# Inverted denominators of a linear attention, spread to 128 partitions by two DMAs per row block instead of four to 32 partitions each

## The chip, the cores and the metric

The kernel runs on one core of one Trainium2 chip. The metric is device time in microseconds (us): the time from the start to the end of one execution, median of several. A profile of one execution is shown beside it; its span runs from the first to the last instruction.

## The reference

One transformer block with adaptive layer norm, on 2048 rows of 1024 (bfloat16 in and out): a linear attention with 32 heads of 32, then a gated MLP of width 3584.

```python
mod = (silu(c) @ w_mod).reshape(1, 6, 1, -1)        # sa, ca, ga, sb, cb, gb
h = layernorm(x) * (1 + ca) + sa
q, k, v = heads(h @ wqkv)                            # 32 heads of 32
phi = lambda t: where(t > 0, t + 1, exp(t)) + 1e-6
pq, pk = phi(q), phi(k)
kv = einsum('bhsd,bhse->bhde', pk, v)
z = einsum('bhsd->bhd', pk)
num = einsum('bhqd,bhde->bhqe', pq, kv)
den = einsum('bhqd,bhd->bhq', pq, z)[..., None] + 1e-6
x = x + ga * ((num / den) merged @ wo)
h = layernorm(x) * (1 + cb) + sb
x = x + gb * ((gelu(h @ w_gate) * (h @ w_up)) @ w_down)
```

What the change touches is the division by `den`: one number for each row and head.

## The kernel before

The rows are worked in four blocks of 512 (`TG`), numbered 0 to 3; blocks 0 and 1 are pair 0, blocks 2 and 3 pair 1. Many of the products are done in seven half-size products instead of eight (the functions built on `seven`), with sums and differences of the operands made on VectorE.

Stages, in program order: layer norm and the products for v and k of all blocks (`kvq_phase`), which leave kv and z summed over all rows; the products for q of pair 0 and then of pair 1 (`q_stages`), which leave phi(q) in `pqT[b]`, laid out as 128 partitions (4 heads of 32 dimensions) by 8 head groups (`KD`) by 512 rows; `merge_phase`, in which kv is multiplied into `wo` (`wp_step`, one head group at a time) beside the last q stages; `wo_phase`, the output projection with the residual: eight row tiles of blocks 0 and 1 by plain products (`wo_tile`, line 1519, 16 matmuls a tile), then blocks 2 and 3 by seven-product stages (`wo_stages`, line 1583), and the second layer norm; then gate, up and down of the MLP for rows 0 to 1023 and 1024 to 2047 (`gate_up`, lines 1698 and 1709, and `down_out`, lines 1914 and 1959).

The division is done on q's side. `den_sums` makes, for a pair of blocks, the denominators of all heads by small matmuls with z (line 1271), takes the logarithm and then the exponential of its negative on ScalarE (lines 1273 and 1274), and stores the inverted denominators (`rdc`, bfloat16) by four DMAs of 16 KB on SP's queue into a DRAM tile, `den_scr` (line 1279). `den_mul` reads them back for one block, so that all 32 partitions of a head hold the same row (line 1289), into an 8 KB buffer per partition, `rden`, and multiplies `pqT[b]` by it in four VectorE instructions of two head groups each. The buffers come from `rden_ring`: blocks 0, 1 and 2 use the same one, block 3 another. The projections wait for these multiplications. All VectorE products and sums of two tensors are issued by the helper `tt_op`, so the profile puts them on line 779.

Nothing is issued in program order. Every instruction is recorded by a planner (`Plan`), with its engine, an assumed cost and what it depends on. The planner orders each engine's instructions by list scheduling with due times; for TensorE it keeps the program's order. `plan.extra` adds to the assumed latency of a DMA, and `plan.together(True)` lets several writes into the same memory lines wait only for the older users of the lines and not for one another. At the end `refine` moves the instructions of each engine by a table written out in the file, `SHIFTS`: one number for each instruction of an engine, which says from which place of the planner's order the one in this place comes (`z4` stands for four zeros). The order that runs is the one after `SHIFTS`.

SP's queue carries nearly all loads: weights, x, the reads of den, and the transposing loads of the second layer norm's rows (`h2_load`, line 1455). POOL's queue carries most stores to DRAM.

Of the kernel before, what the change touches and what calls it, by code (L numbers as in the profile page):

```python
# [11 lines left out]
BF16 = mybir.dt.bfloat16  # L12
# [9 lines left out]
        "z1 4 4 4 4 4 -5 -5 -5 -5 48 -1 -1 -1 -1 -1 -1 -1 -1 -1 -1 -1 -1 -1 -1 -1 -1 7 7 7 7 7 7 7 7 7 7 7 7 7 7 7 7 "  # L22
        "-17 -17 -17 -17 -17 -17 -17 -17 3 3 3 3 -5 -5 -5 -5 8 8 8 8 20 20 20 20 20 20 20 20 20 20 20 20 20 20 20 20 "
        "-20 -20 -20 -20 24 24 24 24 24 24 24 24 24 24 24 24 24 24 24 24 -28 -28 -28 -28 -28 -28 -28 -28 -44 -44 -44 "
        "-44 16 16 16 16 -36 -36 -36 -36 12 12 12 12 12 12 12 12 12 12 12 12 -8 -8 -8 -8 -36 -36 -36 -36 28 28 28 28 "
        "-40 -40 -40 -40 -4 -4 -4 -4 z16 -20 -20 -20 -20 z12 16 16 16 16 16 16 16 16 16 16 16 16 16 16 16 16 16 16 16 "
        "16 16 16 16 16 16 16 16 16 16 16 16 16 -24 -24 -24 -24 -24 -24 -24 -24 -40 -40 -40 -40 -40 -40 -40 -40 8 8 8 8 "
        "8 8 8 8 8 8 8 8 8 8 8 8 -16 -16 -16 -16 -16 -16 -16 -16 z8 16 16 16 16 16 16 16 16 16 16 16 16 16 16 16 16 -16 "
        "-16 -16 -16 -16 -16 -16 -16 8 8 8 8 52 -21 -21 -21 -21 -21 -21 -21 -21 -1 -1 -1 -1 -1 -1 -1 -1 11 11 11 11 11 "
        "11 11 11 28 28 28 28 19 19 19 19 11 11 11 11 20 20 20 20 -25 -25 -25 -25 -25 -25 -25 -25 -25 -25 -25 -25 8 8 8 "  # L30
        "8 8 8 8 8 25 25 25 25 25 25 25 25 13 13 13 13 -37 -37 -37 -37 -37 -37 -37 -37 -3 -3 -3 -3 25 25 25 25 25 25 25 "
        "25 25 25 25 25 25 25 25 25 -32 -8 -8 -8 -8 -32 -32 -32 -32 -40 -40 -40 -40 -16 -16 -16 -16 -12 -12 -12 -12 -20 "
        "-20 -20 -20 40 40 40 40 z4 -8 -8 -8 -8 -4 -4 -4 -4 -4 -4 -4 -4 -4 -4 -4 -4 20 20 20 20 -4 -4 -4 -4 -12 -12 -12 "
        "-12 -8 -8 -8 -8 -8 -8 -8 -8 -8 -8 -8 -8 36 36 36 36 -4 -4 -4 -4 -4 -4 -4 -4 z4 4 4 4 4 -12 -12 -12 -12 -8 -8 "
        "-8 -8 4 4 4 4 8 8 8 8 8 8 8 8 -12 -12 -12 -12 16 16 16 16 z4 12 12 12 12 12 12 12 12 -36 -36 -36 -36 -8 -8 -8 "
        "-8 -16 -16 -16 -16 12 12 12 12 4 4 4 4 -4 -4 -4 -4 8 8 8 8 -16 -16 -16 -16 -4 -4 -4 -4 4 4 4 4 -4 -4 -4 -4 z8 "
        "4 4 4 4 -4 -4 -4 -4 4 4 4 4 -4 -4 -4 -4 z16 4 4 4 4 24 24 24 24 24 24 24 24 -4 -4 -4 -4 -4 -4 -4 -4 -20 -20 "
        "-20 -20 28 28 28 28 20 20 20 20 32 32 32 32 -20 -20 -20 -20 -20 -20 -20 -20 -20 -20 -20 -20 -12 -12 -12 -12 "
        "-12 -12 -12 -12 -12 -12 -12 -12 28 28 28 28 4 4 4 4 -12 -12 -12 -12 -12 -12 -12 -12 16 16 16 16 -4 -4 -4 -4 "
        "-12 -12 -12 -12 12 12 12 12 -8 -8 -8 -8 z4 -20 -20 -20 -20 16 16 16 16 16 16 16 16 16 16 16 16 -8 -8 -8 -8 12 "  # L40
        "12 12 12 -12 -12 -12 -12 -24 -24 -24 -24 8 8 8 8 -20 -20 -20 -20 -4 -4 -4 -4 4 4 4 4 -4 -4 -4 -4 4 4 4 4 -4 -4 "
        "-4 -4 4 4 4 4 -4 -4 -4 -4 z8 32 32 32 32 32 32 32 32 32 32 32 32 -12 -12 -12 -12 -8 -8 -8 -8 -8 -8 -8 -8 -20 "
        "-20 -20 -20 60 60 60 60 60 60 60 60 -16 -16 -16 -16 -24 -24 -24 -24 8 8 8 8 8 8 8 8 8 8 8 8 -28 -28 -28 -28 "
        "-36 -36 -36 -36 -16 -16 -16 -16 -24 -24 -24 -24 8 8 8 8 -12 -12 -12 -12 -12 -12 -12 -12 -12 -12 -12 -12 -12 "
        "-12 -12 -12 12 12 12 12 12 12 12 12 12 12 12 12 12 12 12 12 -24 -24 -24 -24 -12 -12 -12 -12 12 12 12 12 -24 "
        "-24 -24 -24 16 11 11 11 11 -9 -9 -9 -9 -9 -9 -9 -9 9 9 9 9 z5 -14 -14 -14 -14 z24 6 6 6 6 -2 -2 -2 -2 -8 -8 "
        "z10 6 6 6 6 -4 -4 -4 -4 -4 -4 2 2 2 2 2 2 2 2 -8 1 1 1 1 1 1 7 7 7 7 -18 6 6 6 6 -8 -8 -8 -8 2 -9 -9 11 11 11 "
        "11 -4 z4 1 -9 -9 -9 -9 1 1 1 1 -9 32 32 32 32 32 32 32 32 32 32 32 32 32 32 32 32 48 48 48 48 48 48 48 48 24 "
        "24 24 24 -28 -28 -28 -28 -28 -28 -28 -28 -28 -28 -28 -28 -28 -28 -28 -28 -28 -28 -28 -28 4 4 4 4 4 4 4 4 4 4 4 "
        "4 -40 -40 -40 -40 -40 -40 -40 -40 -40 -40 -40 -40 z8 64 64 64 64 4 4 4 4 4 4 4 4 -12 -12 -12 -12 -12 -12 -12 "  # L50
        "-12 4 4 4 4 4 4 4 4 -12 -12 -12 -12 -12 -12 -12 -12 -4 -4 -4 -4 -4 -4 -4 -4 -4 -4 -4 -4 -4 -4 -4 -4 4 4 4 4 4 "
        "4 4 4 -12 -12 -12 -12 -12 -12 -12 -12 z16 8 8 8 8 8 8 8 8 -8 -8 -8 -8 -8 -8 -8 -8 4 4 4 4 -4 -4 -4 -4 z8 44 44 "
        "44 44 24 24 24 24 -8 -8 -8 -8 -8 -8 -8 -8 -4 -4 -4 -4 -12 -12 -12 -12 -4 -4 -4 -4 -12 -12 -12 -12 -8 -8 -8 -8 "
        "16 16 16 16 8 8 8 8 -12 -12 -12 -12 -12 -12 -12 -12 -12 -12 -12 -12 4 4 4 4 -4 -4 -4 -4 8 8 2 2 2 2 4 4 4 4 4 "
        "4 4 4 -14 -14 -14 -14 8 8 8 8 8 8 8 8 -4 -4 -4 -4 -12 -12 -12 -12 20 20 20 20 -4 -4 -4 -4 -4 -4 -4 -4 12 12 12 "
        "12 24 24 -2 -2 -2 -2 -10 -10 -10 -10 10 10 10 10 -22 -22 -22 -22 8 8 32 32 -6 -6 -6 -6 6 6 -16 -16 -16 -16 22 "
        "22 z2 -8 -8 -8 -8 -4 -4 -4 -4 z2 -6 -6 -6 -6 z2 -6 -6 -6 -6 z4 6 6 -2 -2 -2 -2 -2 -2 6 6 6 6 -2 -2 -2 -2 4 4 4 "
        "4 -12 -12 38 38 8 8 8 8 34 34 -4 -4 -4 -4 8 8 4 4 -14 -14 -22 -22 -6 -6 -6 -6 -2 -2 -2 -2 8 8 -22 -22 20 20 20 "
        "20 -6 -6 -12 -12 -12 -12 -10 -10 -10 -10 z6 4 4 4 4 -14 -14 -14 -14 z6 12 12 12 12 -4 -4 -4 -4 32 32 32 32 8 8 "
        "8 8 -12 -12 -12 -12 -12 -12 32 32 -8 -8 -8 -8 -18 -18 8 8 24 24 -2 -2 -12 -12 -12 -12 -12 -12 -12 -12 6 6 6 6 "  # L60
        "z2 -16 -16 -16 -16 8 8 8 8 z4 6 6 6 6 z2 4 4 4 4 4 4 -30 -30 -30 -30 30 30 30 30 -2 -2 -2 -2 10 10 10 10 z2 -4 "
        "-4 -16 -16 -12 -12 -12 -12 24 24 4 4 -4 -4 16 16 -6 -6 -6 -6 -20 -20 -20 -20 z6 12 12 -12 -12 -12 -12 -2 -2 -2 "
        "-2 -2 -2 -2 -2 4 4 -2 -2 -2 -2 6 6 6 6 -4 -4 -4 -4 26 26 26 26 2 2 -10 -10 z6 26 26 -14 -14 -14 -14 22 22 2 2 "
        "-6 -6 -6 -6 -6 -6 -16 -16 -16 -16 z2 -6 -6 -6 -6 8 8 8 8 -8 -8 -8 -8 -4 -4 -4 -4 z2 6 6 6 6 36 36 -2 -2 -8 -8 "
        "-8 -8 z2 -4 -4 26 26 -4 -4 4 4 4 4 -4 -4 30 30 -6 -6 24 24 -16 -16 -16 -16 -4 -4 z2 -12 -12 -12 -12 -10 -10 "
        "-10 -10 2 2 2 2 -4 -4 -10 -10 -10 -10 50 50 -2 -2 -2 -2 2 2 -4 -4 -4 -4 -2 -2 -2 -2 -2 -2 4 4 4 4 30 30 -8 -8 "
# [430 lines left out]
def kernel(  # L497
# [14 lines left out]
    P = 128  # L512
# [6 lines left out]
    KD = D // P  # L519
    JF = F // P  # L520
    TG = 512
# [1664 lines left out]
```

## Time and profile before

| | before |
|---|---|
| median of 3 runs | 738.85 us (738.4 to 741.09) |
| the profiled execution | 740.71 us |
| its span | 738.9 us |
| TensorE (PE) busy | 719.7 us, 97% |
| VectorE (DVE) busy | 655.2 us, 89% |
| ScalarE (ACT) busy | 451.6 us, 61% |
| GpSimd (POOL) busy | 97.8 us, 13% |
| DMA | 159.26 MB in 160956 packets, mean 216 GB/s |
| granted TensorE clock | 1.0 throughout |

PE is matmul and PEld the weight load, which overlaps it. In a timeline a line gives the start and the length in us, the engine, the line of the kernel, the operation, out<-in by tile names, and the number of instructions; the bracket is the idle time just before the first of them and what ended it. The chain of waits follows the work that ended last back from the end, step by step, to what released it; "DMA mem<-den" in it is the time from the issue of a read of den to its landing in SBUF, "DMA den<-mem" that of a store. In the windows view each engine has its busy time and instruction count for a stretch; the last three columns are the granted clock, the mean busy share of the 16 DMA engines, and GB/s.

### The profile page before, as it was taken

How to read it: one execution, taken by the hardware profiler on the slowest of the kernel's cores; microseconds unless marked ns; L12 is line 12 of the kernel's file. 1: busy time of each engine (PE TensorE's matmuls, PEld its weight loads, DVE VectorE, ACT ScalarE, POOL GpSimd, SP SyncE). 2: the span in 40 equal slices, each digit the busy share in tenths (PEclk: the TensorE clock that was granted, in tenths of full speed). 3: DMA queues.
4: the chain of work that ended last, by engine and by line, in shares of the span. 5: the costliest groups of instructions: out<-in, count | busy, mean ns of one | idle time of the engine just before them, and what ended most of it. 6: DMA issues, size and time to landing. Idle time of an engine off the chain costs nothing.

```text
span 738.9 us, 12098 instructions
## 1 busy us (share of the span) xinstructions
PE 719.7 (97%) x4341; PEld 404.2 (55%) x4353; DVE 655.2 (89%) x1469; ACT 451.6 (61%) x823; POOL 97.8 (13%) x174
## 2 busy tenths in 40 slices
PE   4999999999999999999999999999999999999997
PEld 3444444444344455555555576545555555568674
DVE  6799978787789999998998798888898999999998
ACT  4385665669787789999777631017667766753110
POOL 2345542020020101213100000101000000000000
PEclk9999999999999999999999999999999999999999
DMA  9977886986799685666795898753334546599982
GB/s 296 363 209 223 207 156 127 339 283 179 243 271 258 209 279 194 192 203 229 235 202 173 228 288 244 273 186 114 114 91 153 185 161 207 157 240 302 262 270 73
DMA packets 160956, 159.26 MB, mean 216 GB/s; under 512 B 34176, under 2 KB 140416, under 8 KB 160256
## 3 DMA queue, kind: packets, MB, share of 16 engines
q1 hardware_dynamic: 143696, 122.57, 55.9%
q0 software_dynamic: 14848, 33.82, 15.4%
q10 hardware_dynamic: 2352, 2.10, 0.9%
q8 instruction: 34, 0.56, 0.3%
q14 instruction: 26, 0.21, 0.1%
HBM read 122.42 MB, written 36.04 MB: 214 GB/s over the span
## 4 chain that ended last, share of the span: by engine, by line
PE 79%; DVE 12%; DMA 4%; ACT 2%; SPq 1%; issue 1%; DVEq 0%; ACTq 0%
PE psum L1698 33%; PE psum L1959 11%; PE psum L1709 11%; PE psum L1914 9%; DVE mem L779 8%; PE psum L1142 5%; PE psum L1583 3%; PE psum L1212 3%; DMA mem<-den 3%; PE psum L915 2%; DVE mem L857 2%; DMA den<-mem 1%; DVE mem L1062 1%; DVE mem L1081 1%; PE psum L1256 1%
## 5 line engine op out<-in xcount | busy, mean ns | idle before, releaser
L779 DVE TENSOR_TENSOR mem<-mem 128x512 f16<-128x512 f16 (+13 forms) x857 | 376.5, 485 | 15.5 <-DMA mem<-den 4.3
L1698 PE MATMUL psum<-mem 128*128 128x512 f16 x1144 | 275.0, 379 | 0.2
L1086 ACT ACTIVATE mem<-psum 128x512 f32<-128x512 f32 (+3 forms) x320 | 169.0, 556 | 131.8 <-PE psum L1959 45.2
L779 DVE TENSOR_TENSOR mem<-psum,mem 128x512 f16<-128x512 f32 (+5 forms) x213 | 159.3, 756 | 26.9 <-PE psum L1142 5.4
L1698 PEld LDWEIGHTS <-mem 128*128 128x128 f16 (+1 forms) x1144 | 111.8, 98 | 101.3 <-issue 1.5
L1709 PE MATMUL psum<-mem 128*128 128x256 f16 x742 | 108.4, 273 | 0.0
L1709 PEld LDWEIGHTS <-mem 128*128 128x128 f16 (+1 forms) x742 | 72.2, 98 | 44.9 <-DVE psum L779 0.7
L1959 PE MATMUL psum<-mem 128*128 128x256 f16 (+1 forms) x784 | 88.0, 273 | 0.0
L1959 PEld LDWEIGHTS <-mem 128*128 128x128 f16 x784 | 76.7, 98 | 11.7
L1914 PE MATMUL psum<-mem 128*128 128x512 f16 (+2 forms) x348 | 74.9, 370 | 0.6 <-DVE mem L779 0.5
L1142 PE MATMUL psum<-mem 128*128 128x512 f16 (+1 forms) x274 | 62.4, 379 | 0.4
L779 DVE TENSOR_TENSOR psum<-psum,mem 128x256 f32<-128x256 f32 x106 | 44.6, 427 | 13.4 <-ACT mem L1086 12.0
L1914 PEld LDWEIGHTS <-mem 128*128 128x128 f16 x350 | 34.2, 98 | 36.2 <-issue 0.7
L1212 PE MATMUL psum<-mem 128*128 128x512 f16 x224 | 51.7, 379 | 1.5 <-DVE mem L779 1.3
L1142 PEld LDWEIGHTS <-mem 128*128 128x128 f16 x280 | 27.1, 98 | 31.8 <-issue 0.6
L1754 ACT ACTIVATE psum<-psum 128x512 f32<-128x512 f32 x56 | 32.6, 585 | 11.8 <-PE psum L1709 7.7
L1773 ACT ACTIVATE mem<-psum 128x512 f16<-128x512 f32 x56 | 33.1, 598 | 9.1 <-PE psum L1698 9.1
L1715 ACT ACTIVATE psum<-psum 128x256 f32<-128x256 f32 x53 | 19.7, 379 | 30.5 <-PE psum L1709 30.3
L1212 PEld LDWEIGHTS <-mem 128*128 128x128 f16 (+1 forms) x224 | 21.5, 98 | 27.6 <-issue 3.1
L1783 ACT ACTIVATE mem<-mem 128x512 f16<-128x512 f16 x56 | 34.6, 627 | 1.0 <-DVE mem L779 1.0
L1519 PE MATMUL psum<-mem 128*128 128x512 f16 x128 | 28.4, 379 | 1.6 <-DVE mem L779 1.6
L1241 PE MATMUL psum<-mem 128*128 128x512 bf16 x124 | 28.2, 379 | 0.2
(142 smaller groups left out, 569.7 us busy)
## 6 DMA issues: line engine op xcount, KB each, us to landing
mem<-in_B_w_gate_dram SPq DMA_DIRECT2D x14, 1024.0 KB
mem<-in_B_w_up_dram SPq DMA_DIRECT2D x14, 1024.0 KB
mem<-in_w_mod_dram SPq DMA_DIRECT2D x24, 512.0 KB
mem<-us SPq DMA_DIRECT2D x24, 448.0 KB
mem<-ts SPq DMA_DIRECT2D x5, 1792.0 KB
ts<-in_B_w_down_dram POOLq DMA_DIRECT2D x28, 256.0 KB, 5.5
mem<-in_B_w_down_dram SPq DMA_DIRECT2D x15, 448.0 KB
mem<-in_A_x_dram SPq DMA_DIRECT2D x24, 256.0 KB
```

Source lines behind the costliest of these rows:

```text
L779: ve.tensor_tensor(out=out, in0=a, in1=b, op=op)
L1086: ac.activation(out=t, in_=ps, func=AF.Copy)
L1142: te.matmul(ps, lhsT=A[:, k, i * P:(i + 1) * P], rhs=B[:, k, :], start=(start and k == 0), stop=(k == KH - 1), skip_group_check=True)
L1212: te.matmul(o, lhsT=W[:, k, (j0 + i) * P:(j0 + i + 1) * P], rhs=h_form(a, k), start=(start and k == 0), stop=(k == KH - 1), skip_group_che ...
L1519: te.matmul(psw[:, half, :], lhsT=pqT[b][:, g, tl * P:(tl + 1) * P], rhs=Wp[:, g, half * NW:(half + 1) * NW], start=(g == 0), stop=(g == K ...
L1698: te.matmul(ps, lhsT=a[:, k, e, :], rhs=b[:, k, :], start=(start and k == 0), stop=(k == KH - 1), skip_group_check=True)
L1709: te.matmul(ps, lhsT=self.x[a][:, k, :], rhs=self.y[y][:, k, :], start=(start and k == 0), stop=(k == KH // 2 - 1), skip_group_check=True)
L1754: ac.activation(out=z, in_=x, func=AF.Copy)
L1773: ac.activation(out=o, in_=ps, func=AF.Gelu_apprx_tanh)
L1783: ac.activation(out=o, in_=o, func=AF.Gelu_apprx_tanh)
L1914: te.matmul(psm[:, q, c], lhsT=A[:, i, q * P:(q + 1) * P], rhs=wt[:, i, c], start=(start and i == 0), stop=(i == NPR - 1), skip_group_chec ...
L1959: te.matmul(ps[:, q, :], lhsT=a[:, k, q * P:(q + 1) * P], rhs=y[:, k, :], start=(start and q == 0 and k == 0), stop=(k == NPR // 2 - 1), s ...
```

## The change

The tile in DRAM loses its gaps: each head row of a block is now 8 groups by 512 rows in one piece, where 32 elements lay between the groups' rows. `den_mul` reads it by two DMAs, each for four of the eight head groups and for all 128 partitions, with 4 KB a partition in one piece; before, it read it by four, each for the 32 partitions of one head of a group and for all eight head groups, in pieces of 1 KB. The four are no longer marked as belonging together. Neither the stores' number and size nor the multiplications change. `SHIFTS` has new numbers for all five engines; for SP it has eight entries less, 219 for 227.

```diff
 SHIFTS = {
     "PE": (
...
-    den_scr = [scr_pool.tile([2, P // DH, KD, TG + DH], BF16, name=f"den{pr}", tag=f"den{pr}") for pr in range(2)]
+    den_scr = [scr_pool.tile([2, P // DH, KD * TG], BF16, name=f"den{pr}", tag=f"den{pr}") for pr in range(2)]
...
         for b in range(2):
             for half in range(2):
                 o = DH * (2 * b + half)
-                sy.dma_start(out=den_scr[pr][b, :, KH * half:KH * half + KH, 0:TG],
+                sy.dma_start(out=den_scr[pr][b, :, half * KH * TG:(half + 1) * KH * TG].rearrange("j (g t) -> j g t", g=KH),
                              in_=rdc[o:o + KH * P // DH, :])
         plan.extra = 0
 
     def den_mul(b):
         plan.extra = 4000
         rden = rden_ring()
-        plan.together(True)
-        for j in range(P // DH):
-            src = den_scr[b // 2][b % 2, j][:, 0:TG]
-            sy.dma_start(out=rden[DH * j:DH * j + DH], in_=src[None, :, :].to_broadcast((DH, KD, TG)))
-        plan.together(False)
+        for h in range(2):
+            src = den_scr[b // 2][b % 2, :, h * KH * TG:(h + 1) * KH * TG]
+            sy.dma_start(out=rden[:, h * KH:(h + 1) * KH, :].rearrange("p g t -> p (g t)"),
+                         in_=src[:, None, :].to_broadcast((P // DH, DH, KH * TG)))
         plan.extra = 0
```

Here `P` is 128, `DH` 32, `KD` 8, `KH` 4 and `TG` 512.

## The prediction

> **What bounds the kernel now.** I read the page's busy shares and chain first, then the chain in order of time around the denominators, then TensorE's timeline, and last the DMA rate over single stretches.
>
> ```profile
> PE 719.7 (97%) x4341; PEld 404.2 (55%) x4353; DVE 655.2 (89%) x1469; ACT 451.6 (61%) x823; POOL 97.8 (13%) x174
> PE 79%; DVE 12%; DMA 4%; ACT 2%; SPq 1%; issue 1%; DVEq 0%; ACTq 0%
> ```
>
> TensorE is busy 719.7 of 738.9 us, so it sets the end, and only 19.2 us can be won by removing waits. The page puts 3% of the span's chain on the transfer mem<-den, the spread that the change rewrites, and 1% on den<-mem, the small stores ahead of it. Both are on the chain in two places:
>
> ```profile
> 172.26 3.47 DMA den<-mem
> ...
> 177.75 9.28 DMA mem<-den
> ...
> 200.87 3.71 DMA den<-mem
> ...
> 208.14 9.25 DMA mem<-den
> ```
>
> Each stretch runs from the issue of the last read to its landing. What that costs TensorE is in the brackets of its timeline (idle time just before):
>
> ```profile
> 187.81 1.21 PE L1519 MATMUL psum<-mem 128*128 128x512 f16 x4 [0.67 <-DVE mem L779]
> 189.95 4.49 PE L1519 MATMUL psum<-mem 128*128 128x512 f16 x20 [0.94 <-DVE mem L779]
> ...
> 220.67 0.60 PE L1583 MATMUL psum<-mem 128*128 128x512 f16 x2 [0.87 <-DVE mem L779]
> 221.72 1.90 PE L1583 MATMUL psum<-mem 128*128 128x512 f16 x8 [0.45 <-DVE mem L779]
> 223.91 8.38 PE L1583 MATMUL psum<-mem 128*128 128x512 f16 x38 [0.29 <-DVE mem L779]
> ```
>
> Line 1519 is the output projection of blocks 0 and 1, line 1583 that of blocks 2 and 3. The multiplications by the inverted denominators on VectorE (line 779) come late because the spread lands late. The bracketed waits are 0.67 + 0.94 = 1.61 us at the first place and 0.87 + 0.45 + 0.29 = 1.61 us at the second, **3.2 us together**. That is all that a faster spread can win directly: 0.43%.
>
> The rate of the transfers, in the windows view (the last two columns are the DMA engines' busy share and GB/s):
>
> ```profile
> 187.00:189.00 2.00, 1.33 (x5) 0.23 (x4) 1.94 (x4) 2.00 (x3) 0.00 (x0) 1.00 1.02 400
> 210.00:212.00 2.00, 2.00 (x11) 0.90 (x10) 1.98 (x3) 1.42 (x3) 1.26 (x3) 1.00 1.13 221
> ```
>
> In the second stretch the reads of den run: 32 partitions each, in pieces of 1 KB. Sixteen engines, all busy, move 221 GB/s, 14 GB/s each. In the first the last of them are done and weights and x go to 128 partitions in rows of 2 and 4 KB: 400 GB/s, 25 GB/s each.
>
> **The change, part by part.** The bytes stay: a block's spread is 128 partitions of 8 KB, 1.05 MB.
>
> *Issues.* Sixteen reads of den become eight; one took 0.45 us in SP's queue (line 1289), so SP issues 3.6 us less. The eight reads of blocks 2 and 3 are issued over 4.04 us at 204.66 in the SP timeline; four need about 1.8. I count nothing for it: the engines are already full when the later ones are issued. The stores into den (line 1279, 0.6 us each) keep number, 16 KB and shape.
>
> *Waits.* A multiplication of four head groups now needs one DMA, not four, and the next block's first read waits for two multiplications of the old one, not for four (blocks 0, 1 and 2 share one buffer). One multiplication is about 0.64 us (three in 1.90 us at 187.06), so this frees a buffer half 1.3 us earlier. On SP nothing but loads of x and of w_mod stands behind these waits.
>
> *The transfer itself.* This is the term that decides. The new source pattern is 4 rows, each repeated 32 times, with 4 KB in one piece; the destination is 128 partitions. The trace of before has no such read, but it has the stores into den, whose destination is 4 by 4 rows. Its record of semaphore updates shows for such a store one update about 1.0 us after the issue and then only four (1.8 to 2.6 us for the store at 170.22); for a read, which is 8 pieces by 32 partitions, it shows sixteen, one for each engine. So a pattern whose slowest dimension is 4 seems to be served by four engines. I take the new reads to run on four. The Trainium skill, "DMA: Bandwidth & Descriptors", section "Why a DMA increments its semaphore by 16 and not by 1", says the same as a rule: the engine count is the largest number up to 16 that divides the slowest dimension of both patterns, and on SP's queue they are the lowest-numbered engines. By that rule it is 4, and all the new reads share the same four; the store's four updates agree with it.
>
> The price: 512 KB over four engines is 131 KB each. At 25 GB/s (the 4 KB rows) that is 5.2 us, at 14 GB/s 9.4 us. I take 5.2, since the new pieces are 4 KB; 9.4 stays for the range. A block's two reads then take 10.5 us, one after the other, where its 1.05 MB takes 4.7 us at 221 GB/s now: **5.8 us more a block**. The twelve other engines are freer, but every other load has its share on those four.
>
> *The shift table.* It gives each engine's order as moves against the planner's. On TensorE the planner keeps the program's order, so both tables can be read against it, with the lines in the trace's order of weight loads. Only 824 of 4353 slots hold the same matmul, but the phases stand nearly alike: den_sums of pair 0 begins at slot 927, 8 matmuls of 0.217 us (1.7 us) earlier than 935; the output projection begins at 1039 in both, that of blocks 2 and 3 at 1219 in both. What the other engines' orders are worth can't be read so. TensorE has one long wait, of 1.29 us (113.31), outside the start, the end and the two places above, so a new table can win about 1 us at best, and lose as much by the size of such waits: I count 0, with 1.5 us either way.
>
> *The sum, place by place.* Block 0: its last read landed at 187.03. Plus 5.8, minus 1.7 for the earlier den_sums: 191.1. The multiplication of groups 4 and 5 takes 0.64 us, so TensorE's wait that ended at 189.95 ends at about 191.9: **+2**. Block 1: its muls end at 205.1, and its first matmul is tile 4 at 205.6 in the trace. With four engines it lands some 6 us later than its 200 us; its first half, needed first, stays ahead of TensorE, which is itself 2 us later: **0**. Blocks 2 and 3: four reads are 21 us in place of 9.3, so the second block lands near 217.4 + 11.7 + 2 = 231. The first lands near 221, and tile work of block 2 begins at 220.67 + 2: **+1**, if the new order reads block 2 first; block 3 is needed about ten stages' matmuls later, after 231. Behind them on SP stand the two transposing loads of the next stage:
>
> ```profile
> 219.13 13.47 SPq L1455 DMA_TRANSPOSE mem<-xhs  x2
> ```
>
> They now start when den is done on all engines; on four of them they would queue until 231. ScalarE's modulation that needs them begins at 234.11, and TensorE's first matmul of the gate (line 1698) at 244.84 follows it directly. I put 3 us of this delay on TensorE, about half of what the 12 us late engines could cost, since stages of block 3 stand before it as filler: **+3**. Together +6. The profiled execution took 740.71 us (1.8 us more than its span), which gives 746.7; the median of the three runs is 738.85, 1.86 below it. Against the median: **745 us**.
>
> **The rivals.**
>
> *Sixteen engines after all (20 in 100).* If the four rows do not bind the engine count, the spread goes to all partitions at the 400 GB/s row: 1.05 MB in 2.6 us instead of 4.7, the waits of 3.2 us vanish, and the kernel is faster: 735.7 us. For it speaks the 221 against 400 GB/s of the two rows above; against it the four updates of the stores. The point from which it decides is sixteen updates per new read. The Trainium skill, "SBUF — State Buffer", section "Door 1: The DMA port swizzle", gives the reason for the low rate now: partitions 0 to 31 reach 8 of 16 ports. The two rows agree with it.
>
> *Four engines that also get in each other's way (22).* A read to 32 partitions runs now at 14 GB/s an engine though all sixteen work, so the partitions' side limits it. If the four engines walk through their 32 partitions in step and meet at the same place, each read takes 9.4 us, 18.7 a block. Block 0 then lands at 187.03 + 14 - 1.7 = 199.3, 10 us late; block 1 costs 4 more, blocks 2 and 3 with the transposes 10: +24, of which the new order can fill perhaps a quarter: +18, 757 us. The same page says that partitions 32 apart share a port; by that rule engines that start together meet at once. No run here shows it.
>
> *The new order hides it (16).* The spread is on four engines, but den_sums and the reads stand early enough in every queue: the waits of 3.2 us stay or shrink, and the time is 738 to 741. For it speaks that DMA is only 25% busy from 165 to 170 us; against it that den_sums moved just 1.7 us.
>
> **How the numbers follow.** The forecast has 42 in 100 and spans 742 to 750, by the table's 1.5 us and by 0 to 6 us for the transposes. This kernel can be told from no change at about 0.5%, 3.7 us: below 735.2 is faster, above 742.5 slower. Slower: 42 + 22, together 0.64. The first rival lies at the lower bound, so its 20 are 10 faster and 10 within, by the table; of the last's 16, 13 are within and 3 faster: 0.13 and 0.23. The range reaches from the first rival's time to a little above the second's: 735.5 to 760.
>
> **What would show it.** Right: the reads of den, eight of 512 KB, with five updates each; DMA share below 0.6 while they run alone; waits of VectorE for mem<-den above 4.3 us; TensorE's idle time before lines 1519, 1583 or 1698 above 3.2 us together. Wrong: sixteen updates a read and GB/s near 400 in that stretch (first rival); a read of 9 us or more (second); TensorE's idle time unchanged (third).

## The result, and the profile after

| | before | after |
|---|---|---|
| median | 738.7 us (738.4 to 741.09) | 764.55 us (761.74 to 765.91, 4 runs) |
| span of the profiled execution | 738.9 us | 764.1 us |
| TensorE busy / idle in the span | 719.7 / 19.2 us | 727.3 / 36.8 us |
| VectorE's waits for mem<-den | 4.3 us | 25.4 us |
| first matmul of the gate in TensorE's timeline (line 1698 before, 1702 after) | 244.67 us | 268.13 us |
| last read of den landed | 217.4 us | 244.2 us |

The ratio, estimated over all runs of both, is 1.0338, 95% interval [1.0302, 1.0374]: slower by 3.4%. The prediction said 745 us and a range of 735.5 to 760; the direction held and the size didn't.

The span grew by 25.2 us, and two numbers make that up: TensorE's idle time grew by 17.6 us, and its busy time by 7.6 us for the same 4353 matmuls (the profile of before has 4341 of them on record; kernels of the experiments with all 4353 at full clock are busy for 719.7 to 720.7 us, so the missing records hardly count). In the code after, the store into den is line 1284, the read 1293, `tt_op` 784, the projections 1523 and 1587. The page of after, busy times, granted clock in 40 slices, and the chain by engine:

```profile
PE 727.3 (95%) x4353; PEld 405.9 (53%) x4353; DVE 655.0 (86%) x1469; ACT 452.5 (59%) x823; POOL 99.6 (13%) x174
...
PEclk9999999999898999999999999999999999999999
...
PE 75%; DVE 10%; DMA 10%; SPq 2%; ACT 1%; issue 1%; ACTq 0%; DVEq 0%
```

DMA's share of the chain went from 4 to 10% (mem<-den alone from 3 to 8%), and two slices show a clock below nine tenths where before all showed nine or more. The chain in order of time, at the denominators:

```profile
177.62 18.64 DMA mem<-den
...
198.66 15.14 DMA mem<-den
...
220.23 23.93 DMA mem<-den
```

Before there were two such pieces, of 9.3 us each; now there are three, of 15 to 24 us. TensorE's timeline, the groups with idle time ahead of them:

```profile
191.03 1.04 PE L1523 MATMUL psum<-mem 128*128 128x512 f16 x4 [1.76 <-DVE mem L784]
198.69 5.80 PE L1523 MATMUL psum<-mem 128*128 128x512 f16 x20 [6.63 <-DVE mem L784]
...
215.71 18.77 PE L1523 MATMUL psum<-mem 128*128 128x512 f16 x80 [3.22 <-DVE mem L784]
...
242.57 3.46 PE L1587 MATMUL psum<-mem 128*128 128x512 f16 x8 [8.01 <-DVE mem L784]
246.67 17.74 PE L1587 MATMUL psum<-mem 128*128 128x512 f16 x80 [0.64 <-DVE mem L784]
```

The brackets add up to 20.3 us, against 3.2. The rate of the reads where nothing else runs, in the windows view (the last three columns are the granted clock, the share of the 16 DMA engines, and GB/s):

```profile
194.00:196.00 2.00, 0.00 (x0) 0.00 (x0) 0.00 (x0) 0.00 (x0) 0.00 (x0) 0.64 0.26 104
196.00:198.00 2.00, 0.00 (x0) 0.00 (x0) 1.69 (x4) 0.00 (x0) 0.00 (x0) 0.50 0.26 103
...
236.00:238.00 2.00, 0.00 (x0) 0.00 (x0) 0.00 (x0) 0.00 (x0) 0.00 (x0) 1.00 0.26 104
```

A share of 0.26 is four engines of sixteen, at 26 GB/s each: a read of 512 KB takes 5.1 us. The record of semaphore updates shows for each new read one update about 1 us after its issue and then four. So the reads run on four engines, at the price that the prediction took. What was wrong is what that price does to the kernel.

### The profile page after: what moved, and what is told of

It is laid out like the page before. It is cut to its first block, busy times and chain, and to the rows that moved or that the text cites. A ratio compares the mean times of both kernels' runs of the same rounds, so it can differ in the third digit from the quotient of the medians.

```text
span 764.1 us, 12082 instructions
## 1 busy us (share of the span) xinstructions
PE 727.3 (95%) x4353; PEld 405.9 (53%) x4353; DVE 655.0 (86%) x1469; ACT 452.5 (59%) x823; POOL 99.6 (13%) x174
## 4 chain that ended last, share of the span: by engine, by line
PE 75%; DVE 10%; DMA 10%; SPq 2%; ACT 1%; issue 1%; ACTq 0%; DVEq 0%
PE psum L1702 32%; PE psum L1713 10%; DVE mem L784 9%; DMA mem<-den 8%; PE psum L1147 7%; PE psum L1963 7%; PE psum L1918 7%; PE psum L1217 4%; PE psum L1246 3%; PE psum L1587 3%; DMA mem<-in_w_mod_dram 3%; PE psum L1261 1%; ACT mem L1091 1%; DVE mem L2135 1%; PE psum L920 0%
## 5 line engine op out<-in xcount | busy, mean ns | idle before, releaser
L784 DVE TENSOR_TENSOR mem<-mem 128x512 f16<-128x512 f16 (+12 forms) x857 | 377.4, 483 | 40.9 <-DMA mem<-den 25.4
L1702 PE MATMUL psum<-mem 128*128 128x512 f16 x1144 | 275.1, 379 | 0.6 <-DVE mem L784 0.3
L784 DVE TENSOR_TENSOR mem<-psum,mem 128x512 f16<-128x512 f32 (+6 forms) x213 | 159.7, 755 | 29.8 <-PE psum L1217 7.2
L1217 PE MATMUL psum<-mem 128*128 128x512 f16 x224 | 52.8, 388 | 0.0
L1523 PE MATMUL psum<-mem 128*128 128x512 f16 x128 | 31.0, 404 | 11.6 <-DVE mem L784 11.6
L1217 PEld LDWEIGHTS <-mem 128*128 128x128 f16 (+1 forms) x224 | 22.0, 100 | 26.9 <-issue 3.2
L1587 PE MATMUL psum<-mem 128*128 128x512 f16 x112 | 26.9, 395 | 8.8 <-DVE mem L784 8.6
```

The source lines that it names most:

```text
L784: ve.tensor_tensor(out=out, in0=a, in1=b, op=op)
L1217: te.matmul(o, lhsT=W[:, k, (j0 + i) * P:(j0 + i + 1) * P], rhs=h_form(a, k), start=(start and k == 0), stop=(k == KH - 1), skip_group_che ...
L1587: te.matmul(ps, lhsT=A[:, k, i * P:(i + 1) * P], rhs=B[:, k, :], start=(start and k == 0), stop=(k == KH - 1), skip_group_check=True)
L1702: te.matmul(ps, lhsT=a[:, k, e, :], rhs=b[:, k, :], start=(start and k == 0), stop=(k == KH - 1), skip_group_check=True)
```

## The experiments

All runs, with the time at which the last read of den landed (issue plus the time to the last semaphore update, in the profiled execution). The edits are shown shortened to what is issued in the end; three dots and words in an index stand for what is left out. e11, e12, e13 and e15 read rows of a weight matrix in place of the denominators, so they leave the division out and serve for timing alone. The ratio is against the kernel before in the same job (its medians: 738.9 to 739.8 us).

| run | median us | ratio | last read landed |
|---|---|---|---|
| e1 four reads of 32 partitions, new order | 741.39 | 1.0030 [1.0011, 1.0049] | 215.5 |
| e4 four engines, old order | 770.53 | 1.0425 [1.0409, 1.0441] | 244.3 |
| e3 eight engines, new order | 747.13 | 1.0111 [1.0078, 1.0143] | 226.0 |
| e10 sixteen engines, new order | 742.62 | 1.0035 [1.0011, 1.0059] | 217.1 |
| e5 the change, block 2 first | 767.15 | 1.0392 [1.0372, 1.0411] | 245.5 |
| e8 the change, block 0 first | 765.61 | 1.0358 [1.0341, 1.0375] | 243.2 |
| e9 the change, filler matmuls, one group misplaced | 770.76 | 1.0425 [1.0407, 1.0442] | 244.6 |
| e14 the change, both waits filled | 765.12 | 1.0341 [1.0308, 1.0374] | 244.2 |
| e11 four engines, each row read once | 763.13 | 1.0322 [1.0302, 1.0341] | 239.3 |
| e12 32 partitions, each row once | 742.08 | 1.0048 [1.0033, 1.0063] | 214.5 |
| e13 sixteen engines, each row once | 740.49 | 1.0018 [1.0004, 1.0032] | 213.2 |
| e15 plain load of 128 rows | 740.79 | 1.0009 [0.9994, 1.0024] | 213.9 |
| e6 before, block 2 first | 738.97 | 0.9998 [0.9985, 1.0012] | 215.6 |
| e7 before, block 0 first | 738.60 | 0.9997 [0.9983, 1.0012] | 214.8 |

None is faster than the kernel before; e6, e7 and e15 are level with it.

### The engines or the order: e1, e4

The change has two parts, the new reads and the new shift table. e1 keeps the table and undoes the reads:

```diff
-            sy.dma_start(out=rden[:, h * KH:(h + 1) * KH, :]...,
-                         in_=src[:, None, :].to_broadcast((P // DH, DH, KH * TG)))
+            for j in range(P // DH):
+                src = den_scr[b // 2][b % 2, j, h * KH * TG:(h + 1) * KH * TG]
+                sy.dma_start(out=rden[DH * j:DH * j + DH, h * KH:(h + 1) * KH, :]...,
+                             in_=src[None, :].to_broadcast((DH, KH * TG)))
```

> The order of the changed kernel is kept for every engine; each of its eight reads of den is issued as four reads of 32 partitions with 4 KB pieces (slowest dimension 32). Theory A, the engine count: the new reads cost what they do because their source's slowest dimension is 4 and four DMA engines serve them. Then each read here gets sixteen updates, the 4 x 512 KB of blocks 2 and 3 land within about 10 us of the first issue instead of 27.8, TensorE's waits before the two output projections fall from 20.3 us to under 5, the clock stays up, and the time is 738 to 745. Theory B, the new shift table: the order is worse by itself. Then the time stays above 755.

Measured: 741.39 us, sixteen updates a read, VectorE's waits for den 2.4 us. The reads of pair 1 landed 13.3 us after their first issue, not the 10 expected. The engine count is worth 23 of the 25.8 us (764.55 less 741.39); the new table with reads of the old width costs about 2. Its window while the reads of pair 1 run:

```profile
209.00:215.00 6.00, 6.00 (x30) 2.73 (x28) 4.92 (x8) 4.89 (x12) 1.63 (x4) 1.00 0.98 234
```

e4 is the other half: before's table and the change's reads (the first two of the four slots of each block; the other two issue nothing).

```diff
-            sy.dma_start(out=rden[DH * j:DH * j + DH], in_=src[None, :, :].to_broadcast((DH, KD, TG)))
+            if j < 2:      # half j of the block, all 128 partitions
+                src = den_cp[b // 2][b % 2, :, 0, j * KH * TG:(j + 1) * KH * TG]
+                sy.dma_start(out=rden[:, j * KH:(j + 1) * KH, :]..., in_=src[:, None, :].to_broadcast((4, 32, KH * TG)))
```

> The kernel before with its own order; at the places of its four reads of a block the two reads of the change are issued (and two places stay empty), on a copy of den without gaps. Theory A: slower than before by 15 to 35 us, since a block's two reads take 10.3 us alone on four engines instead of 4.7, with waits at the same two places. Theory B: within 4 us of before.

Measured: 770.53 us, 6 us more than with the new table. So the new order does absorb 6 us of what the slow spread costs. In its TensorE timeline one wait, for block 2, stands out, and the 80 matmuls behind it run partly at the half clock (19.86 us, where the change has 17.74):

```profile
247.45 19.86 PE L1597 MATMUL psum<-mem 128*128 128x512 f16 x80 [17.48 <-DVE mem L783]
```

### Eight engines: e3

Two copies of each row: the matmul that sums the denominators gets its columns twice, the store writes 32 rows, and a read has 8 rows repeated 16 times.

```diff
-                         in_=src[:, None, :].to_broadcast((P // DH, DH, KH * TG)))      # 4 rows, 32 times
+                         in_=src[:, None, :].to_broadcast((8, 16, KH * TG)))             # 8 rows, 16 times
```

> The order of the changed kernel; z's columns are filled twice, so that every store writes two copies of each row of den (32 rows, 32 KB) and a read's source is 8 rows repeated 16 times. Two reads a block as in the change. Theory A: eight engines, nine updates a read, a read alone about 2.6 us at 206 GB/s and 0.5 DMA share; the time lies near the kernel before, 738 to 748. If 128 partitions and 4 KB pieces, not the engine count, were what is slow, it would stay at 764.

Measured: nine updates a read (1 and 8), 747.13 us. Eight engines are half way, but not twice as fast as four:

```profile
213.00:217.00 4.00, 4.00 (x20) 1.80 (x19) 3.14 (x5) 3.61 (x8) 0.00 (x0) 1.00 0.51 139
```

139 GB/s is 17 an engine, where four had 26 each. Engines that get in each other's way were the second rival. Something of the kind shows at eight and not at four; what slows the eight, no run here separates.

### Moving the work in time: e5, e8

If the price were that a block is late for its first use, it should help to bring the block that is needed first. e5 exchanges blocks 2 and 3 in SP's reads and VectorE's multiplications:

```diff
+            if e == "SP":   put([tags["read", b, i] for b in (2, 3) for i in range(2)])
+            if e == "DVE":  put([tags["mul", b, g] for b in (2, 3) for g in (0, 2, 4, 6)])
```

> The changed kernel with one move in the order: SP reads block 2 before block 3, and VectorE multiplies block 2 before block 3 (the eight places of these multiplications stay). The prediction put 1 us on blocks 2 and 3 if block 2 is read first; in the changed kernel block 3 is read first and TensorE waits 8.65 us for block 2. Theory A with that step as its main error: 750 to 756, the wait before line 1587 gone or moved to block 3 by under 3 us. If the transposing loads behind the reads set the place anyway: 760 or more, with the wait moved to the first matmul of the gate.

Measured: 767.15 us, no gain, and no wait at the gate either. VectorE's timeline shows why: it takes its work in order, and stands at the multiplications of the block that lands last before it can go on.

```profile
238.97 1.90 DVE L793 TENSOR_TENSOR mem<-mem 128x1024 bf16<-128x1024 bf16 x3 [5.14 <-DMA mem<-den]
245.56 0.69 DVE L793 TENSOR_TENSOR mem<-mem 128x1024 bf16<-128x1024 bf16 x1 [3.11 <-DMA mem<-den]
```

e8 moves block 0's two stores and two reads, on SP, ahead of the six loads between them:

```diff
+            if e == "SP":
+                first = [tags["store", 0, 0], tags["store", 0, 1], tags["read", 0, 0], tags["read", 0, 1]]
+                seqs[e][lo:hi] = first + [op for op in seqs[e][lo:hi] if op not in first]
```

> The changed kernel (four engines), in which SP issues block 0's two stores and its two reads of den ahead of the six loads of x and of w_mod that stand between them; nothing else is moved. My theory: in the changed kernel the two reads of block 0 landed 14.3 and 18.6 us after their issue because they stand behind those loads in SP's queue and share their four engines with them; with the loads behind them each read has its four engines nearly to itself, so the block lands some 7 to 8 us earlier (near 188 to 190 in place of 196.3). TensorE's two waits before the output projection of blocks 0 and 1 (1.76 and 6.63 us) fall to 2 to 3 us together, the half-clock stretch behind them goes, and the time falls by 5 to 8 us, to 757 to 760. Rival A: the reads are slow there for their own sake (the destination, not the queue), they take 14 us or more wherever they stand, and the time stays at 763 to 766. Rival B: the loads that are now late hold TensorE elsewhere (x or w_mod missing before a matmul at 195 to 215), the gain is given back, and the time is 762 to 768 with new waits for loads in the trace.

Measured: 765.61 us. Block 0 did land 6.7 us earlier (189.6 for 196.3), and TensorE's first two waits fell from 8.39 to 2.73 us. Nearly all of it was given back one block later, where the wait was 3.22 us and is now 8.32:

```profile
192.01 6.18 PE L1531 MATMUL psum<-mem 128*128 128x512 f16 x20 [2.73 <-DVE mem L789]
...
214.50 19.96 PE L1531 MATMUL psum<-mem 128*128 128x512 f16 x80 [8.32 <-DVE mem L789]
...
241.52 3.59 PE L1595 MATMUL psum<-mem 128*128 128x512 f16 x8 [6.99 <-DVE mem L789]
```

Block 1 landed at 212.6 (213.8 in the change), the last read at 243.2 (244.2): the same. My theory was wrong in its reason, too: with nothing ahead of them in the queue the reads still landed 12.5 and 16.9 us after issue. The loads that are issued behind them slow them all the same: pieces of 4 KB took a median of 290 to 341 ns at 176 to 184 us. Whether the loads' share of the four engines or the slower pieces make up the delay isn't shown, since the record names no engine for a piece. Rival B named the outcome, but the new waits are for den, not for x or w_mod.

What e5 and e8 share is that the last read lands at 243 to 246 us whatever the order. By this account the four engines are full. In the change:

```profile
DMA packets 6001, 12.38 MB, mean 170 GB/s; under 512 B 2044, under 2 KB 2157, under 8 KB 5997
...
mem<-den SPq DMA_DIRECT2D x8, 512.0 KB
```

These two lines are the DMA view from 172 to 245 us. Eight reads of 512 KB over four engines are 256 pieces of 4 KB each, 40.7 us at the 159 ns that a piece takes undisturbed. The other 8.2 MB (x, w_mod, stores, a transposing load), if they are spread evenly over all sixteen, are 0.51 MB each, another 20 us at that rate. That is an estimate of 61 of the 73 us; pieces that were slowed (below) take part of the rest. In the windows of 2 us from 172 to 245 the share falls below 0.25, which is four engines of sixteen, only once (0.22 at 216 to 218).

The reads of pair 1 also start late, as SP's timelines of before and after show:

```profile
204.66 4.04 SPq L1289 DMA_DIRECT2D mem<-den  x8
```

```profile
216.40 4.51 SPq L1293 DMA_DIRECT2D mem<-den  x4
```

TensorE comes to the sums of pair 1 (line 1276) behind the first 24 matmuls of block 0's projection, at 205.09 instead of 194.37; then the 16 KB stores, which four engines serve as well, land 4.9 to 8.6 us after their issue instead of 1.8 to 3.7. e8 tells which of the two binds: there the sums come 6.3 us earlier, at 198.78, but the stores take 5.2 to 13.9 us and the reads start at 215.42, only 1.0 us earlier. So the queue on the engines holds them, more than TensorE's order.

### The clock: e9, e14

Behind the long waits the granted clock is half. In the windows above it drops at 194.6 (0.64 over 2 us); the same view gives 0.62 for 238 to 242 and 0.53 for 242 to 246, and the 8 matmuls at 242.57 take 3.46 us where 8 take 1.9 elsewhere. In the clock record of the change the half-clock stretches begin at 143.37, 194.57, 215.05 and 238.94 us and last 3.41 or 6.83; the starts lie 15, 6 and 7 steps of 3.41 us apart. In the 3.41 us ahead of each, TensorE was busy 40, 27, 25 and 0% of the time; ahead of 191.15 it was busy 48% and kept its clock (44% in e1). The Trainium skill, "TensorE: Matmul & The Clock Gate", section "What's actually happening", says that the clock is halved after an idle window of about 3.4 us and comes back after about 3.4 us of work, with windows that run freely. The length of the windows and their running freely agree with these rows; that a window must be idle throughout does not: behind the wait of 2.06 us that ended at 142.03 TensorE had already worked for 1.3 us when the clock dropped.

Is this part of the loss, or does it only fill time in which TensorE would wait? Filler matmuls keep TensorE busy, 29 ahead of the fifth matmul of tile 0 and 35 (e9) or 33 (e14) at the start of block 2's part:

```diff
+    def filler(op, ps, n):
+        for _ in range(n):
+            nc.tensor.matmul(ps, lhsT=ident, rhs=selb..., start=True, stop=True)
+        nc.tensor.matmul(*op.args, **op.kw)
```

> The changed kernel with 64 matmuls more, whose result nobody reads: 29 ahead of the fifth matmul of the output projection's tile 0 (where TensorE waits 6.63 us for block 0's denominators) and 35 ahead of the first matmul of block 2's part of it (where it waits 8.01 us). They cost nothing if they lie in the waits. My theory: the waits are followed by some 7 us at a granted clock of half, because TensorE was idle before (194.6 to 201.4 and 238.9 to 245.8 in the changed kernel). Kept busy, the clock stays at 0.98 or more there, the matmuls behind the waits run at full speed, and the time falls by 2 to 4 us, to 760.5 to 762.5; the third stretch (215.0 to 218.5) stays. Rival: the half clock costs nothing, since the matmuls of these stretches wait for the multiplications by the inverted denominators anyway: the clock is full and the time is unchanged within 0.8 us (763.5 to 765.5). A time above 766 would mean that the added matmuls are longer than the waits.

Measured: 770.76 us. The second group stood four matmuls too late: behind the wait, not in it. It took 8.2 us there and made the time 6.2 us longer than the change's, so this run tells only of the first place, where the 20 matmuls ended about 1 us earlier than in the change. e14 puts the group right:

> The changed kernel with matmuls more whose result nobody reads: 29 ahead of the fifth matmul of tile 0, as before, and 33 ahead of the very first matmul of block 2's projection; in the earlier run the second group stood four matmuls too late, behind the wait, and cost its whole 8.2 us. Theory: both long waits are filled, the granted clock stays at full there, the 20 and 88 matmuls behind the waits run at 0.22 us each from the first on, and the time falls by 2 to 4 us against the change, to 760.5 to 762.5. Rival: the half clock costs nothing since other waits follow: 763.5 to 765.5.

Measured: 765.12 us, as the change (764.55). Both waits are filled and the clock is full at 194 to 198 and 238 to 244. The 20 matmuls at block 0 end 1.4 us earlier, and the next wait, 3.22 us in the change, is 4.55. At the second place the wait comes back behind the fillers:

```profile
234.65 7.28 PE L1305 MATMUL psum<-mem 128*128 128x512 f16 x33
242.46 0.39 PE L1307 MATMUL psum<-mem 128*128 128x512 f16 x1 [0.53 <-DVE mem L787]
...
246.65 1.87 PE L1607 MATMUL psum<-mem 128*128 128x512 f16 x4 [2.29 <-DVE mem L787]
```

The last read landed at 244.15 again. The clock was half for 3.41 us behind the wait at block 1 (215.86), which nothing filled, and, other than expected, for 3.41 us behind this last one (246.58). There it did delay the rest: the gate's first matmul came at 269.48, 1.35 us later than in the change. Without that the profiled span of 765.5 us would be about the change's 764.1, so the full clock ahead of the landing still gained nothing. The rival holds: the half clock ahead of a landing isn't the cause of the longer time. TensorE runs slowly towards a wait that ends when the last read lands.

### What the old waits were worth: e6, e7

The prediction held that the 3.2 us of waits in the kernel before are all that a faster spread can win. Two kernels remove them by order alone, e6 at the second place (block 2 first on SP and VectorE, as e5) and e7 at the first (block 0's stores, two loads, its reads, then the rest):

```diff
+                rest = [op for op in seqs["SP"][lo:hi] if op not in first + reads]
+                seqs["SP"][lo:hi] = first + loads[:2] + reads + loads[2:] + [op for op in rest if not op.load]
```

> The kernel before (four reads of 32 partitions each), in which SP reads the denominators of block 2 ahead of those of block 3, and VectorE multiplies block 2 ahead of block 3; nothing else is moved. TensorE needs block 2 first, at 220.67, and waits there 0.87 + 0.45 + 0.29 = 1.61 us. My theory from the same exchange in the changed kernel, which gained nothing: VectorE takes its work in order and stands at the multiplication of the block that lands last, so the waits move by at most 1 us and the time stays within 0.3% (737 to 741). Rival: block 2 is there 4 to 5 us earlier, the three waits vanish, and the time is 1.3 to 1.6 us less (737.2 to 737.5, ratio 0.998).

> The kernel before, in which SP issues the two stores of block 0, two of the loads, the four reads of block 0, and then the rest of that stretch; nothing else is moved. The last read of block 0 landed 9.3 us after its issue, at 187.03, beside loads of x and of w_mod, and TensorE waited 0.67 + 0.94 = 1.61 us for it at 187.8 to 190. My theory: the block lands 2 to 3 us earlier, the two waits vanish, and the time is about 1.6 us less (737.2, ratio 0.998). Rival: the loads that now stand behind come late, and TensorE waits for x or w_mod instead; no change or up to 2 us more (739 to 741).

Measured: 738.97 and 738.60 us, ratios 0.9998 and 0.9997. The waits did vanish from the traces: e6's TensorE has none left at block 2's projection (it starts at 218.32 there), and in e7, of all the projections' waits, this one is left, 0.29 where block 2's place had 1.61 though nothing was moved there:

```profile
221.33 15.28 PE L1594 MATMUL psum<-mem 128*128 128x512 f16 x70 [0.29 <-DVE mem L787]
```

The intervals end at 0.9985 and 0.9983, which is 1.1 and 1.3 us: the whole 1.6 us of either place lies just outside. So not even these waits seem to be worth their length. Where they are given back stays open; it may also be that they are shorter in most executions, since the 3.2 us were read from one that took 1.86 us more than the median.

### What limits sixteen engines: e10, e12, e13, e15, and e11

The first rival was that the spread would run on sixteen engines at 400 GB/s. e10 makes it so: four copies of each row in DRAM, 16 rows repeated 8 times, each store issued twice.

```diff
-                         in_=src[:, None, :].to_broadcast((P // DH, DH, KH * TG)))      # 4 rows, 32 times
+                         in_=src[:, None, :].to_broadcast((16, 8, KH * TG)))             # 16 rows, 8 times
```

> The changed kernel with four copies of each row of inverted denominators in DRAM (two from the matmul that sums them, two from storing twice, so eight stores of 32 KB a pair of blocks in place of four of 16 KB); a read has 16 rows, each repeated 8 times, and 128 partitions. Sixteen engines should serve it (seventeen updates a read). Theory, the partitions bind: the reads go to all partitions on all engines, at 370 to 400 GB/s and 159 to 170 ns a piece of 4 KB, a read takes 1.3 to 1.5 us and a block under 3; the waits for den on TensorE are below 2 us and the time is 738 to 741 (ratio 0.998 to 1.003), a little below the 741.4 of the reads of 32 partitions. Rival, reading the same rows over and over binds: 220 to 240 GB/s and 260 to 310 ns a piece, as with 32 partitions; the time is 741 to 744.

Measured: sixteen updates a read (without the early one that I had counted), 742.62 us. The four reads of pair 1 land within 6.4 us of the first, 2.1 us each, or 245 GB/s: hardly more than reads of 32 partitions have (234). Its time is that of e1, with reads as wide and as few as the change's: so it is the engine count that costs the 23 us. But neither the engine count nor the 32 partitions alone explains the low rate. Three runs with rows of wqkv in place of the denominators take the repeats away and vary the pattern:

```diff
+                src = A_wqkv.rearrange("(j k) n -> j k n", j=4)[j, 32 rows, 0:2048]      # e12: four reads of 32 partitions
+                src = A_wqkv.rearrange("(m k) n -> m k n", m=16)[:, 8 rows, 0:2048]      # e13: 16 groups of 8 partitions
+                src = A_wqkv[128 rows, 0:2048]                                           # e15: a plain load
```

> The changed order with each read as four reads of 32 partitions (sixteen engines), as in the run with 741.4 us, but from 32 different rows of wqkv in place of one row 32 times; the denominators are left out of the multiplication and the reads don't wait for their stores. There a piece of 4 KB took 282 ns, 234 GB/s. Theory, the repeated source binds: 159 to 180 ns and 360 to 400 GB/s in the stretch where block 2's and 3's reads run alone. Rival, the 32 partitions bind: 270 to 300 ns and 220 to 240 GB/s again. The time is 739 to 742 either way.

> The changed order, each read one DMA of 16 groups of 8 different rows of wqkv to the 128 partitions (4 KB each, no row twice); the denominators are left out of the multiplication and the reads don't wait for their stores. The run with 16 copied rows repeated 8 times moved 245 GB/s (2.1 us from one read to the next) on sixteen engines, where loads of w_mod move 400. Theory, the way in which the engines walk over the partitions binds (each engine takes 8 adjacent ones, and some meet): again 2.0 to 2.2 us a read and 230 to 260 GB/s. Rival, reading the same rows again and again binds: 1.3 to 1.5 us a read and 350 to 400 GB/s. The time is 738 to 742 either way.

> As the run before, but each read is one DMA of 128 adjacent rows of wqkv, a plain load in two dimensions like those of w_mod; the denominators are left out. Theory: 1.3 to 1.5 us a read, 350 to 400 GB/s, 159 to 170 ns a piece of 4 KB, and TensorE has next to no wait before the output projections: the time is what the new order gives with a spread that costs almost nothing, 738 to 741. Rival, something else than pattern and source binds in that stretch (other transfers, the destination): 2 us a read again.

All four at the same place, while block 0's spread runs beside loads of x and w_mod, in the order e10, e12, e13, e15 (windows view):

```profile
180.00:184.00 4.00, 4.00 (x20) 1.79 (x19) 1.81 (x4) 4.00 (x6) 0.00 (x0) 1.00 1.01 266
```

```profile
180.00:184.00 4.00, 4.00 (x20) 1.84 (x19) 1.81 (x4) 4.00 (x7) 0.00 (x0) 1.00 0.98 234
```

```profile
180.00:184.00 4.00, 4.00 (x20) 1.83 (x19) 2.11 (x4) 4.00 (x7) 0.00 (x0) 1.00 1.06 240
```

```profile
180.00:184.00 4.00, 4.00 (x20) 1.86 (x19) 2.59 (x4) 3.80 (x4) 0.00 (x0) 1.00 0.99 362
184.00:188.00 4.00, 4.00 (x21) 1.78 (x19) 3.07 (x5) 4.00 (x7) 0.00 (x0) 1.00 1.02 409
```

All engines are busy in all four; only the plain load goes beyond, 362 GB/s here and 409 in the next 4 us. In the stretch of pair 1 the median 4 KB piece takes 159 ns in e15, 207 to 234 in e13, 266 to 273 in e12 and 179 to 285 in e10 from 208 us on (the trace's record of packets, in windows of 2 or 3 us). The pattern does slow the pieces (e13 against e15, both with every row once to 128 partitions; what differs is 16 groups of 8 rows against 128 adjacent ones), and the repeated rows add something at most (e10 against e13). In e15 a read landed 1.2 to 1.3 us behind the one before it where they stood in a row, as its theory had it. In my expectation of e13 the walk was to give 230 to 260 GB/s and the repeats nothing; it was 1.8 us a read, between theory and rival, so both have a part. The Trainium skill, "DMA: Bandwidth & Descriptors", section "The descriptor swizzle", says that in a plain transfer to 128 partitions each engine writes one port of its own. That would agree with e15; which partitions an engine gets in the other patterns, no run here shows.

And e15's time answers the first rival: with a spread that costs next to nothing and no wait ahead of the projections, the new order takes 740.8 us. The one long wait left is at the products of kv, which the new order has and the old one hasn't:

```profile
143.28 0.68 PE L1264 MATMUL psum<-mem 128*128 128x129 f16 x9 [2.06 <-DVE mem L787]
```

e11 asks the same of the change itself, with 4 groups of 32 different rows (four engines still):

```diff
+                src = A_wqkv.rearrange("(j k) n -> j k n", j=4)[:, 32 rows, 0:2048]
+                sy.dma_start(out=rden[:, h * KH:(h + 1) * KH, :]..., in_=src)
```

> The changed kernel, whose eight reads take 128 different rows of wqkv (4 groups of 32 rows, not adjacent, 4 KB each) in place of 4 rows 32 times each, so the denominators are left out of the multiplication and the reads don't wait for their stores to land; everything else is as in the change. The source's slowest dimension is still 4, so four engines and five updates a read, 5.1 us alone. It asks why pieces of all loads take 165 ns (2 KB) and 310 ns (4 KB) while a read of den runs beside them, and 84 and 159 ns otherwise. Theory, the repeated source: with rows read once the pieces beside the reads take 84 to 100 and 159 to 180 ns, block 0's reads land 9 to 12 us after issue instead of 14 to 19, and the time falls to 755 to 760. Rival, the engines or the partitions: the pieces stay at 150 to 170 and 290 to 310 ns, block 0's reads take 13 to 18 us, and the time stays at 760 to 766 (a little less than the change for the waits for stores that are gone).

Measured: 763.13 us. The pieces beside the reads still took a median of 152 ns (2 KB, at 176 to 180) and 294 (4 KB, at 180 to 184), against 84 and 159 without a spread beside them, and block 0's reads 14.4 and 18.6 us. The rival holds: with four engines the source's repeats hardly matter.

## Why the prediction was wrong in size

*The engine count* was right: eight reads of 512 KB, five updates each, a share of 0.26. *The price of a read* was right: 5.2 us said, 5.1 measured where it runs alone.

*The sum, place by place, is the step that failed.* It took each block's landing of before and added 5.8 us for its own two reads. But four engines serve all eight reads and, by the even spread, a quarter of every load besides, and hardly a window between 172 and 245 us leaves them free: what one block takes later, the next one finds. Eight reads at 5.2 us are 42 us, with the loads' share some 61 of those 73; the 42 alone, set against the 42 us from the first issue to the last landing before (175.75 to 217.39), would have shown that there was no room. In the slower kernels the delay of the last landing gives the time itself within some 2 us: in the profiled executions 26.8 us in the change (244.2 against 217.4) for 25.2 us of span, 8.6 in e3 for 7.0, 26.9 in e4 for 28.3, 21.9 in e11 for 20.9.

By its places: *Block 0, +2*: landing said 191.1, measured 196.3, and TensorE waits 6.8 us more. The 1.7 us taken off for the earlier den_sums weren't there: they began at 168.04, 1.05 later than before (166.99), behind the wait and the half clock at 142 to 147. The stretch beside loads was priced as if the engines had only den to move, and pieces there take twice as long. *Block 1, 0*: its second read is issued at 198.66, because the buffer half comes free only after block 0's multiplications, and lands at 213.8, where "some 6 us later than its 200" was said; TensorE waits 3.2 us. *Blocks 2 and 3, +1*: the condition "if the new order reads block 2 first" doesn't hold. Both orders read block 3 first, and e5 shows that the condition itself was beside the point: VectorE in order stands at whichever is last. The last landing was 244.2 where 231 was said: from the first issue it took 27.8 us, 15.0 more than before (204.66 to 217.39) where the sum added 11.7, and the reads started 11.7 us later than before (216.40 against 204.66) where it allowed 2. That start is the larger part of the miss, and it is what the blocks ahead handed on. TensorE waits 8.65 us there, 7.0 more than before. *The transposing loads, +3*: they do start late, but SP waits there for the stores of the rows they read (xhs<-mem, 23.4 us in all, 15.4 before), not for den:

```profile
237.11 20.32 SPq L1459 DMA_TRANSPOSE mem<-xhs  x2
```

But TensorE has no wait at the gate (line 1702): everything ahead of it is as late as they are. *The shift table, 0 within 1.5*: it costs about 2 us in e1, and saves about 6 when the spread is slow (e4 against the change).

*The clock* wasn't priced at all. It is most of the 7.6 us of busy time: TensorE worked 12.1 us in the four half-clock stretches, which would take 6.0 at full clock. 1.7 of the 6.0 us lost lie behind the wait for kv at 142.03, which belongs to the order and not to den (e15 has it too); the rest, where e14 filled the waits, was no cause.

Of the rivals: sixteen engines was wrong for this change, and its 735.7 us too, since e10 and e15 run at 742.6 and 740.8. Engines in each other's way came nearest by its time (757), by a mechanism that isn't there with four engines: its sign, a read of 9 us or more, shows nowhere that a read runs alone (5.0 to 5.1 us). The order hides part of it, as the third had it, but a small part.

## What to carry to other kernels

Before a transfer is rewritten into fewer and larger DMAs, look at how many engines will serve it: a source whose outer dimension is 4 had four here, and 4 KB pieces didn't make up for it. When a transfer is bound to few engines, sum up all that these engines have to carry over the whole phase, the loads' share included, and compare that with the phase; prices added block by block miss what the queue hands on. A move in the order that only brings one block forward can give the time back at the next, as it did here.

## What the runs showed of the hardware that wasn't expected

A spread slows the loads beside it though they use other engines as well: 4 KB pieces of all DMAs took a median of 306 ns at 182 to 184 us in the change, against 159 at 176 to 178, with all sixteen engines busy at 233 against 401 GB/s. Four engines that write 128 partitions have 26 GB/s each, eight 17, sixteen 15 (e10), and in plain loads of the same size up to 26 (e15, 409 GB/s). The clock halves without a long idle gap: between 110 and 270 us of all the traces here, a window of 3.41 us at full clock in which TensorE was busy 40% or less was followed by the half clock, and one with 44% or more was not.
